# A delta-rule attention and a gated feed-forward layer on one core: the hand-over order of 1879 tasks is replaced by another

## The chip, the cores and the metric

The kernel runs on one core of one Trainium2 chip. The metric is the device time of one execution in microseconds (us). Three runs of the kernel before took 671.13, 673.59 and 679.51 us, so the median is 673.59 us.

A core has five engines that run side by side, each through its own instructions in program order: TensorE (PE in the profile, with its weight loads as PEld), VectorE (DVE), ScalarE (ACT), GpSimd (POOL) and SyncE (SP), which here only issues DMA transfers. An engine that reaches an instruction whose input is not there waits, and all that stands behind it on that engine waits too.

## The reference

```python
# q, k, v: (4, 8, 768, 48); beta: (4, 8, 768)
k_n = k / (np.linalg.norm(k, axis=-1, keepdims=True) + 1e-06)
state = np.zeros((B, H, D, D))
for t in range(S):
    y[:, :, t] = np.einsum('bhd,bhde->bhe', q[:, :, t], state)
    v_old = np.einsum('bhde,bhd->bhe', state, kt)
    state = state + bt[..., None] * np.einsum('bhd,bhe->bhde', kt, vt - v_old)
x = y.transpose(0, 2, 1, 3).reshape(B * S, H * D)     # (3072, 384)
h = x @ w_in                                          # w_in (384, 2048)
out = (h * np.cos(h)) @ w_out                         # w_out (2048, 384)
```

The first half is a recurrence over 768 time steps for 32 pairs of batch and head; the second half is a feed-forward layer with the gate h cos(h). The weights arrive as 64-bit numbers and are narrowed on the chip.

## The kernel before

**Attention, chunk by chunk.** Time is cut into 24 chunks n of 32 steps. For a chunk, TensorE makes the gram matrix of keys with keys and queries (`gram`, L546), sends keys and queries through the state (`state`, L713), multiplies with an inverted triangular matrix (`solve`, L776), updates the state (`update`, L799), forms the output inside the chunk (`within`, L816) and transposes it into features for the feed-forward layer (`features`, L835). These products work on pieces of 48x32, 64x64 or 32x32 rows and columns of the array, the others on 128x128. Between them DVE and ACT carry results out of PSUM: `gram_keys` and `gram_queries` (L557, L580), `right` (L728), `solve_out` (L786), `update_out` (L807), `within_out`, `features_out`.

**The inverse.** The triangular matrices of chunks 2m and 2m+1 are inverted together. The gram goes to DRAM (`gram_put`, L598), comes back in another layout (`gram_get`, L619), is inverted on POOL in seven tasks `inv m,0` to `inv m,6` (L656 and L663; the one of m = 0 runs on DVE), goes to DRAM (`put`, L677) and comes back as `zt` by `get` (L696), which `solve` of the two chunks needs. These transfers are issued by SP, as are the loads of keys, queries and values and the stores.

**Feed-forward, pair by pair.** Each pair p of chunks gives 256 rows. For p = 0 and 1 the hidden layer is plain (`hidden p,f`, L856, 24 matmul instructions each); for p = 0 the output is plain too (`out 0,i,k`, L1001). Later pairs use a scheme with seven products in place of eight: `layer p,s,i` (L975) for the hidden layer and `out p,step,part` (L1058) for the output, with `left`, `layer_out` and `collect` on DVE and ACT as the additions around it. The gate is `turns` (ACT, L896), `rest` (DVE, L903), `cos` (ACT, L912) and `gate` (DVE, L915).

**Weights.** 28 slabs t are loaded (`weights`, SP), narrowed by `split` (ACT), `shift` (DVE) and `add` (POOL, L438). Slabs 0 to 11 are `w_in`, three for each quarter of the hidden layer; `hidden 0,6` is the first to need slabs 9 to 11. Slabs 12 to 27 are `w_out`; `out 0,0,k` needs those up to 15 + 4k, so `out 0,0,3` needs slab 27.

**The order.** All of this is registered as 1879 tasks by `Order.add`, each with the engine, what it depends on, and the tiles that it makes and uses. `Order.LINE` is a string with all task numbers in one sequence, and `Order.run` emits the tasks in that sequence. An engine gets its own tasks in the sequence's order, and a last loop pins every instruction behind the one before it on its engine, so nothing is reordered later. The number of buffers of each kind of tile is fixed: one PSUM tile (two banks) for the attention's small products (`two`), one for `p_kq`, three banks for the hidden layer (`h`), two places of `p_out` for the output, eight buffers `g` in SBUF that gates, weight slabs and some others share.

```python
line = [keys[int(i)] for i in self.LINE.split()]
for key in line:
    emit, deps, makes, uses = self.tasks[key]
    assert deps <= done, key
    ...
    emit()
```

## Time and profile before

| what | value |
|---|---|
| median of three runs (lowest, highest) | 673.59 us (671.13, 679.51) |
| span of the profiled execution, first to last instruction | 670.2 us |
| TensorE busy | 616.5 us, 92% of the span |
| DVE, ACT, POOL busy | 466.5, 242.4, 347.1 us |
| mean granted TensorE clock | 0.995 |
| HBM read, written | 39.24, 10.75 MB |

The span leaves out what lies around the program on the device; the page gives no separate time for it, and the fastest of the three runs is 0.9 us above the span. Most of TensorE's idle time lies in the first 100 us: it is nearly gapless from there to the end.

### The profile page before, as it was taken

Reading aid. Unit: us, or ns where it says so; the run is one execution under the profiler, and the core shown is the slowest. Engines: PE = TensorE matmul, PEld = TensorE weight load, DVE = VectorE, ACT = ScalarE, POOL = GpSimd, SP = SyncE. Lnnn points to the kernel's source line nnn. Section 1 sums busy time; section 2 is a strip of 40 time slices with the busy share of each in tenths; the row PEclk is TensorE's granted clock in tenths of the full one; section 3 lists DMA queues with packets and bytes.
Section 4 is the critical chain, followed back from the end, with each engine's and each line's share of the span. In section 5 each row is a group of like instructions: output and inputs, shape, how many; then the busy total and the mean of one; then the engine's idle time right before and its main releaser. Section 6 shows DMA issues by size and latency. Waiting matters only on the chain.

```text
span 670.2 us, 27723 instructions
## 1 busy us (share of the span) xinstructions
PE 616.5 (92%) x12120; PEld 580.5 (87%) x12120; DVE 466.5 (70%) x892; ACT 242.4 (36%) x416; POOL 347.1 (52%) x734
## 2 busy tenths in 40 slices
PE   4326789999999999999999999999999999999996
PEld 3225779976889999999999999999999999999996
DVE  6872698897577777787767767777776666656662
ACT  3441565650223433334334332333323333332420
POOL 4268778988728658238458484385383382000000
PEclk9999899999899999999999999999999999999999
DMA  8776594464364523544443624623312302000000
GB/s 179 183 177 156 130 228 124 105 110 66 53 103 68 85 54 57 89 88 70 70 83 55 108 35 73 106 39 53 69 27 39 68 2 40 20 2 24 1 25 24
DMA packets 215645, 51.80 MB, mean 77 GB/s; under 512 B 207076, under 2 KB 210420, under 8 KB 215524
## 3 DMA queue, kind: packets, MB, share of 16 engines
q1 hardware_dynamic: 212516, 49.16, 38.0%
q8 instruction: 95, 1.56, 1.0%
q10 hardware_dynamic: 2752, 0.43, 0.4%
q0 software_dynamic: 256, 0.44, 0.2%
q14 instruction: 26, 0.21, 0.1%
HBM read 39.24 MB, written 10.75 MB: 75 GB/s over the span
## 4 chain that ended last, share of the span: by engine, by line
PE 79%; DMA 7%; SPq 4%; POOL 4%; DVE 2%; issue 2%; ACT 0%; ACTq 0%; DVEq 0%; POOLq 0%
PE p_h L975 28%; PE p_out L1058 27%; PE p_h L856 5%; PE p_kq L713 4%; PE p_out L1001 3%; PE p_u L776 3%; PE p_s L799 3%; PE p_kq L816 2%; PE p_g L546 2%; POOL z L663 2%; DMA pairs<-in_moe_w_in_dram 2%; POOL part L656 2%; PE p_o L1058 2%; DMA qp<-in_q_dram 1%; SPq L310 1%
## 5 line engine op out<-in xcount | busy, mean ns | idle before, releaser
L656 POOL TENSOR_TENSOR part<-z,gb 128x126 f32<-128x126 f32 (+22 forms) x341 | 134.6, 395 | 116.1 <-DMA gb<-g_dr 75.0
L663 POOL TENSOR_TENSOR z<-z,part 128x126 f32<-128x126 f32 (+22 forms) x341 | 138.7, 407 | 26.7
L975 PE MATMUL p_h<-x_ffn,w_in 128*128 128x128 f32 x1120 | 143.0, 277 | 0.0
L975 PEld LDWEIGHTS p_h<-x_ffn,w_in 128*128 128x128 f32 x1120 | 134.2, 192 | 1.5
L1058 PE MATMUL p_out<-w_out,g_ffn 128*128 128x192 f32 x672 | 121.8, 330 | 2.0 <-issue 2.0
L1058 PEld LDWEIGHTS p_out<-w_out,g_ffn 128*128 128x128 f32 x672 | 108.7, 191 | 3.3 <-issue 2.1
L896 ACT ACTIVATE turns<-p_h,quarter_turn 128x512 int32<-128x512 f32 x96 | 65.8, 688 | 105.6 <-DVE p_h L994 72.1
L912 ACT ACTIVATE turns<-turns,halfpi 128x512 f32<-128x512 f32 x96 | 68.7, 721 | 64.3 <-DVE turns L903 63.7
L1058 PE MATMUL p_out<-w_sum,g_ffn 128*128 128x192 f32 x496 | 88.7, 329 | 0.0
L903 DVE SCALAR_TENSOR_TENSOR turns<-p_h,turns 128x512 f32<-128x512 f32 x96 | 65.3, 683 | 22.0 <-ACT turns L896 22.0
L1058 PEld LDWEIGHTS p_out<-w_sum,g_ffn 128*128 128x128 f32 x496 | 79.7, 190 | 0.8
L991 ACT COPY g_ffn<-p_h 128x512 f32<-128x512 f32 x60 | 35.0, 584 | 108.8 <-PE p_h L975 108.7
L1074 DVE TENSOR_TENSOR g_ffn<-g_ffn 128x512 f32<-128x512 f32 x88 | 62.3, 715 | 10.0 <-PE p_out L1058 8.9
L915 DVE TENSOR_TENSOR g_ffn<-turns,p_h 128x512 f32<-128x512 f32 x96 | 64.6, 677 | 6.6 <-ACT turns L912 6.5
L994 DVE TENSOR_TENSOR p_h<-g_ffn,p_h 128x512 f32<-128x512 f32 x60 | 41.5, 692 | 30.5 <-PE p_h L975 23.7
L467 POOL TENSOR_TENSOR knrm<-ksum,halves 128x16 f32<-128x16 f32 (+1 forms) x14 | 36.2, 2590 | 41.5 <-DVE ksum L455 41.5
L1108 DVE SCALAR_TENSOR_TENSOR o<-p_out,o 128x192 f32<-128x192 f32 x74 | 25.2, 353 | 35.4 <-PE p_out L1058 33.9
L856 PE MATMUL p_h<-x_ffn,w_in 128*128 128x128 f32 x384 | 47.3, 282 | 2.3 <-POOL part L656 2.1
L856 PEld LDWEIGHTS p_h<-x_ffn,w_in 128*128 128x128 f32 x384 | 45.8, 197 | 3.3 <-issue 2.2
L975 PE MATMUL p_h<-x_sum,in_sum 128*128 128x128 f32 x320 | 41.6, 277 | 0.0
L786 DVE TENSOR_TENSOR u<-p_u,bz 128x384 f32<-128x384 f32 x48 | 24.4, 550 | 21.9 <-PE p_u L776 21.8
L975 PEld LDWEIGHTS p_h<-x_sum,in_sum 128*128 128x128 f32 x320 | 38.7, 192 | 0.5
(110 smaller groups left out, 767.2 us busy)
## 6 DMA issues: line engine op xcount, KB each, us to landing
pairs<-in_moe_w_in_dram SPq DMA_DIRECT2D x12, 512.0 KB
pairs<-in_moe_w_out_dram SPq DMA_DIRECT2D x16, 384.0 KB
gb<-g_dr SPq DMA_DIRECT2D x22, 256.0 KB
vp<-in_v_dram SPq DMA_DIRECT2D x96, 48.0 KB
out_dram<-o SPq DMA_DIRECT2D x23, 192.0 KB
kp<-in_k_dram SPq DMA_DIRECT2D x128, 24.0 KB
z_dr<-z SPq DMA_DIRECT2D x11, 256.0 KB
zt<-z_dr SPq DMA_DIRECT2D x88, 32.0 KB
```

The costliest lines, as they stand in the source:

```text
L467: nc.gpsimd.tensor_tensor(out=scales[m][2][:, part], in0=sums[m, part.start][:, 0:n], in1=halves[:, 0:n], op=ALU.pow,)
L656: eng.tensor_tensor(out=part, in0=z[:, 0:rows, j, None].to_broadcast(shape), in1=a[:, j, None, j + 1 :].to_broadcast(shape), op=ALU.mult,)
L663: eng.tensor_tensor(out=behind, in0=behind, in1=part, op=ALU.subtract)
L856: nc.tensor.matmul(p_h[:, i], w_in[:, t, (4 * k + i) * 128 : (4 * k + i + 1) * 128], xts[p][:, t, unit * 128 : (unit + 1) * 128], start=(t ...
L896: nc.scalar.activation(turns[p, f], hidden_of(p, f), AF.Identity, bias=quarter_turn, scale=TURN)
L903: nc.vector.scalar_tensor_tensor(out=r, in0=hidden_of(p, f), scalar=TURN, in1=t, op0=ALU.mult, op1=ALU.subtract,)
L912: nc.scalar.activation(r, r, AF.Sin, bias=halfpi, scale=2.0 * math.pi)
L915: nc.vector.tensor_tensor(out=place(p, f), in0=step_of(rests.pop((p, f)), f), in1=step_of(hidden_of(p, f), f), op=ALU.mult,)
L975: nc.tensor.matmul(p_h[:, e], in_sum[:, odd_tile, 4 * s + e] if a == "s" else w_in[:, a, f * 128 : (f + 1) * 128], x_sums[p][:, unit] if b ...
L994: nc.vector.tensor_tensor(out=block(p, s, 0, 1) if i == 3 else p_h, in0=block(p, s, *one), in1=p_h, op=ALU.add,)
L1058: nc.tensor.matmul(p_o, left(p, part, a)[:, e % 4], right(e, b), start=(e == 0), stop=(e == FT // 2 - 1), skip_group_check=True,)
L1074: nc.vector.tensor_tensor(out=left(p, s, to), in0=left(p, s, one), in1=left(p, s, two), op=op)
```

## The change

Only the string `LINE` is replaced. Every task, its instructions, its dependences and all buffers are as before; the tasks stand in another sequence, which came out of a new annealing run that was told the length of TensorE's switches between kinds of products and which buffer each tile gets.

```diff
     LINE = """
-0 1767 1 2 14 10 11 12 3 7 4 37 5 42 15 72 6 38 13 39 16 43 73 40 1768 1771 17 44 19 96 75 1769 97
...
-1759 1758 1743 1760 1763 1761 1762 1764 1765 1766
...
+1741 1744 1739 1748 1671 1740 1746 1749 1750 1743 1751 1753 1756 1752 1754 1755 1757 1759 1745 1747
+1758 1760 1763 1764 1761 1765 1762 1766
 """
```

Translated back to task names, these are the places that matter later on.

TensorE, from chunk 0's update to the eleventh feed-forward task:

```
before  update 0, within 0, gram 4, features 0, state 1, solve_half 1, hidden 0,0, between 1, solve 1,
        update 1, within 1, turn 5, hidden 0,2, gram 5, state 2, features 1, turn 6, hidden 0,4,
        out 0,0,0, solve 2, hidden 0,6, update 2, within 2, hidden 0,8, features 2, hidden 0,10, ...
after   update 0, within 0, gram 4, state 1, features 0, solve_half 1, between 1, solve 1, hidden 0,0,
        update 1, hidden 0,2, within 1, turn 5, gram 5, hidden 0,4, state 2, features 1, hidden 0,6,
        turn 6, hidden 0,8, solve 2, update 2, within 2, hidden 0,10, features 2, hidden 0,12, ...
```

POOL, from the first slab to slab 27 (`norms` is a power on POOL, 1.7 to 3.3 us):

```
before  add 0, norms 1, norms 1, add 1 2 3 5 4, norms 2, inv 1,0-1, add 6, inv 1,2-3, add 7, inv 1,4, add 10,
        inv 1,5-6, add 13 8 12 14 15 9 11, norms 3, add 16 17, inv 2,0-1, add 18 19 20, inv 2,2-3, norms 4,
        add 22 21, inv 2,4, add 24 23, inv 2,5, add 26 25 27, inv 2,6, norms 5, inv 3,0 ...
after   norms 1, norms 1, add 0, norms 2, add 5 3 2 6 1 4, inv 1,0-3, add 7, inv 1,4-5, add 8, inv 1,6,
        add 10 11 9, norms 3, add 14 16, inv 2,0, add 12 13, inv 2,1, add 15, inv 2,2, add 17 18 20 19 21,
        inv 2,3-4, add 22 23, inv 2,5-6, add 25 26 24 27, inv 3,0 ...
```

In the middle part, gram and state products, which stand apart before (`state 8` and `gram 11` with a feed-forward product between them), stand side by side in seven more places (`gram 10, state 8, gram 11`). The seven output products of a pair and the eight layers of the next are interleaved in another rhythm: in 13 places a single short layer (8 matmul instructions) stands between the end of one output product and the start of the next; before, in one place. On SP the stores, loads and the transfers of the inverse pass one another in many places.

## Prediction

> **What bounds the kernel now.** First the busy time by stretches (PE, PEld, DVE, ACT, POOL in us, then the granted clock, the DMA share, GB/s):

> ```profile
> core 0: us, PE busy (x) PEld busy (x) DVE busy (x) ACT busy (x) POOL busy (x), PEclk, DMA share, GB/s
> 0.00:66.00 66.00, 28.16 (x843) 23.47 (x844) 42.48 (x118) 22.78 (x41) 37.68 (x58) 1.00 0.76 173
> 66.00:100.00 34.00, 28.14 (x707) 25.15 (x707) 26.62 (x43) 19.80 (x37) 25.71 (x41) 0.95 0.77 180
> 100.00:143.00 43.00, 42.73 (x834) 39.66 (x833) 37.41 (x67) 25.92 (x48) 36.72 (x62) 1.00 0.50 108
> ...
> 165.60:168.40 2.80, 0.85 (x16) 0.67 (x5) 1.71 (x2) 0.00 (x0) 2.33 (x7) 1.00 0.20 30
> 168.40:171.90 3.50, 3.50 (x72) 2.95 (x71) 0.34 (x1) 0.00 (x0) 2.95 (x8) 0.51 0.34 59
> ...
> 216.00:430.00 214.00, 214.00 (x4382) 205.74 (x4381) 159.53 (x304) 78.41 (x132) 121.64 (x280) 1.00 0.44 74
> ```

> TensorE is full from 100 us to the end but for three short stalls; before that it idles some 44 us. So the change can act in three ways: the start, TensorE's own length, and stalls.

> Next the chain of waits between 60 and 100 us (start, length, what), which says what held the start back:

> ```profile
> 83.13 5.14 DMA z_dr<-z
> ...
> 97.45 0.89 PE p_s L799 x32
> ```

> Before this stands an unbroken row of `POOL part L656` and `POOL z L663`: inverse 1, ended at 83.1, then `put 1`, `get 2`, and chunk 2's update at 97.45, with TensorE gapless afterwards. POOL's waits show what interrupts it there:

> ```profile
> POOL w_in L438 <- DVE w_in L434: 19.4, 5, 12.4
> ...
> POOL w_out L438 <- DVE w_out L434: 5.9, 5, 1.9
> ```

> Last the chain between 505 and 560 us, for the price of a switch:

> ```profile
> 514.39 0.72 PE p_g L546 x49
> ...
> 516.33 2.80 PE p_out L1058 x16
> 519.13 0.84 PE p_g L546 x62
> ...
> 521.06 2.60 PE p_out L1058 x16
> ...
> 547.96 1.31 PE p_kq L713 x85
> 549.27 1.50 PE p_out L1058 x8
> ```

> The same 16 instructions take 2.80 after a product on small pieces and 2.60 after a 128x128 one; every other product shows this 0.20. A gram with its state behind it takes 516.33 - 514.39 = 1.94; apart they take 0.84 and 1.31.

> **TensorE's own length.** Decoding both strings, TensorE changes between piece sizes 185 times before and 173 times after; gram and state stand side by side in 11 places before, 18 after. One joining saves 0.84 + 1.31 - 1.94 = 0.21 and one 0.20: 0.41 by these pieces, 0.35 by starts in the timeline, so seven save 2.5 to 2.9. Going the other way, one more visit to 32x32 and one `update` parted from its `within` cost 0.2 each. Laid end to end with the row's durations, the products from `out 0,0,3` to the end come to 513.2 before and 510.4 after: **-2.8**. No trace shows a state followed at once by the next gram; if that saves only the 0.20, the term is -1.7; at most it is -3.2.

> **The start.** The first stretch hardly moves. The DVE order puts `sum 0,1` ahead, which starts `norms 0` some 2 us later (10.9 for 9.1), but `gram_keys 0` waited to 13.3 anyway; both gram transfers leave some 0.4 us earlier; two DVE tasks (`gram_queries 2` 0.41, `scale 1,1` 1.0) now stand before inverse 0's last task, so `put 0` leaves at about 36.0 (35.5 before); `get 0` no longer queues behind `gram_get 1` on SP and leaves at 39.4 (40.6). `solve_half 0` comes to about 44.8 (46.0).

> Then POOL decides. Seven slabs now precede inverse 1 on POOL; their `shift`s stand on DVE behind inverse 0 (34 to 35 us), so inverse 1 starts at about 50.5 for 47.9. From there to the end of `add 27` POOL took 140.9 - 47.9 = 93.0. The new order puts `inv 2,6` in front of it (6.4 + 0.6 idle), takes `norms 4` (2.9) and `add 6` (1.3) out, and with slabs prepared early most of 9.6 us in which POOL waited for slabs between (2.9, 1.7, 1.9, and several of 0.8) can go: I take 6.8. That gives 93.0 + 7.0 - 4.2 - 6.8 = 89.0, so slab 27 at 139.5, and `out 0,0,3`, which needs it, at 139.9 for 142.9: **-3.0**. TensorE's path agrees: slabs 10, 11, 9 follow inverse 1 (50.5 + 28.0 + 2.6 for two slabs + idle = 81.8, three slabs: 85.8), releasing `hidden 0,6`; from it to `out 0,0,3` are 51.7 of products and one wait of 1.2 for `solve_out 2`, together 138.7. Bounds: none of POOL's waits saved, 146.3 and +3.4; all saved, TensorE's own path, 138.7 and -4.2.

> **Stalls that go.** `out 1,1,0` stood still from 166.07 for 1.95 with nothing to wait for ("issue"), and the trace has a packet of the instruction queue at 165.1, just before; the next 3.5 us ran at a clock of 0.51, and products there are 1.9 longer. This hangs on where TensorE is in its code, not on an order that I can read: I count half, **-1.9**. `solve 6` and `solve 16` waited 1.57 and 0.99 for `zt`, and products around them took 2.0 longer (`solve 6` 1.36 for 0.73): **-4.5** if both go. By the new positions `zt` of chunk 6 is there 5.7 before its solve.

> [...]

> **Stalls that come.** (a) `zt`. Chunk 8's solve moves 6.4 of work later, but `gram_keys 9` now follows `layer_out 2,0,4` on DVE, and `gram_put 9` queues on SP behind `get 6`, `get 7` and `blocks 10`. With `gram_get 4` at 191.5, 4.8 to inverse 4, 28.0 for it and two `norms` of 2.9 that now stand inside, `put 4` leaves at 230.9; 5.5 to `get 8` and 3.8 to use give 240.2, and TensorE wants it at 139.9 + 99.0 = 238.9: a wait of 1.3. The same walk leaves chunks 18 and 22 within a microsecond of waiting, the others 3 to 7 spare. I take two waits of 1.3 with 0.6 of slower products each: +3.8, between 0 and 8. (b) Cover behind products. For each product I compared the work between it and the product whose result it needs through DVE or ACT with the durations on that way plus 0.2 for each hand-over. After `out 0,1,3` the margin is under 0.5 us in 8 places before, in 44 after: the joined grams have 1.16 of cover for 1.24 (a gram must wait until DVE has read the other out of `two`), 13 output products have 0.89 for 0.75 of `collect`, in one place before. The 8 places waited 0.0. What can spoil it is a DVE task in front: DVE is busy 159.53 of 214. As none of the 8 waited, I take 0.05 each: +2.2; ends 0 and, at 0.3 each, 13. Together **+6.0**.

> **Sum.** 670.2 - 2.8 - 3.0 - 1.9 - 4.5 + 6.0 = 664.0 for the profiled span. The median stands 3.4 above that span (673.59 to 670.2), so 667.4: I predict **667 us**. ACT and the remaining SP moves count nothing: ACT is busy 36%, stores are waited for by nobody until the last, whose place is unchanged.

> **Rivals.**
> - *The start gains all and nothing comes back*: 670.2 - 4.2 - 2.8 - 3.9 - 4.5 + 3.4 = 658.2. For it: POOL's waits in the start are real. Against: 36 new tight places. 0.20.
> - *Only the switches count*, POOL's waits stay, stalls move: 673.6 - 2.2 = 671.4. For it: POOL's path to slab 27 is 7.0 longer. 0.20.
> - *Lost cover makes it slower*: one DVE task of 0.68 in front in all 44 places is 30 us, 697. It decides (over 687) from 20 / 44 = 0.45 us a place. For it: `scale 9` (1.1 to 1.5) now stands right before `right 13`, whose solve has 0.13 of margin. Against: the 8 places of before. 0.12.
> - *Forecast*: 0.48.

> The range 656 to 682 takes in the first two rivals and (b)'s upper half. Under 2% from 673.6, 660.1 to 687.1, a measurement of this kernel hardly tells a change from none. The first rival falls mostly below: faster 0.20; forecast and second within: 0.69; slower 0.11.

> **What would show it.** Right: `add 27` ends near 139.5 and `out 0,0,3` starts near 140; TensorE busy from there some 2.8 shorter; no wait at `solve 6`; in TensorE's waits a few entries for `zt` and small ones for `g`/`tt` (L580) and `o` (L1108). Wrong: `add 27` after 143, or waits for DVE adding to over 10 us after 160, or an idle start much shorter than 40 us.

## The result and the profile after

The kernel after takes 705.8 us (median of four runs, 704.25 to 709.49), the kernel before 674.32 beside it (four runs): **1.051 times as long, interval 1.046 to 1.057**. Another pair of runs on another chip gave 1.045 (1.041 to 1.049). The forecast was 667, the range ended at 682.

First the busy time by stretches of the kernel after (PE, PEld, DVE, ACT, POOL in us, then the granted clock, the DMA share, GB/s). The third and fourth row are one stand-still and the 3.5 us behind it:

```profile
core 0: us, PE busy (x) PEld busy (x) DVE busy (x) ACT busy (x) POOL busy (x), PEclk, DMA share, GB/s
0.00:66.00 66.00, 24.93 (x776) 20.88 (x776) 38.65 (x111) 21.63 (x40) 34.15 (x53) 0.99 0.73 172
66.00:100.00 34.00, 29.59 (x704) 27.08 (x688) 21.14 (x40) 17.93 (x34) 26.39 (x47) 0.81 0.63 140
...
444.88:447.12 2.24, 0.01 (x2) 0.00 (x0) 2.14 (x8) 1.44 (x2) 0.00 (x0) 1.00 0.47 68
447.12:450.60 3.48, 3.48 (x32) 3.31 (x32) 1.05 (x3) 0.00 (x0) 0.00 (x0) 0.52 0.16 24
216.00:430.00 214.00, 200.89 (x4053) 192.97 (x4057) 146.76 (x277) 69.04 (x117) 124.44 (x286) 0.96 0.40 66
```

In the stretch from 216 to 430 us, where TensorE was busy for all 214.00 before, it now stands still for 13.1 and gets through 4053 matmul instructions in place of 4382. DVE and ACT are less full than before, POOL is hardly fuller (124.44 for 121.64). TensorE's waits behind 148 us (engine, line, what was late; us in total, times, longest) say that nothing was late:

```profile
PE p_g L544 <- issue: 9.1, 4, 2.5
PE p_kq L711 <- issue: 8.4, 5, 2.6
PE p_out L1056 <- issue: 3.0, 2, 2.0
PE p_out L1056 <- ACT g_ffn L989: 2.3, 1, 2.3
PE p_u L774 <- issue: 1.5, 2, 1.3
...
```

Before, the same view has two lines:

```profile
PE p_u L776 <- DMA zt<-z_dr: 2.6, 2, 1.6
PE p_out L1058 <- issue: 2.0, 1, 2.0
```

"Issue" is a wait for nothing that the profile shows. After, there is no entry for `zt`, and none for DVE. The one entry for ACT is of the same kind, as its place below tells. The chain of waits shows one of them from near (start, length, what): a gram, a state, and a stop inside the second gram.

```profile
442.47 0.72 PE p_g L544 x49
...
443.25 1.16 PE p_kq L711 x68
444.41 0.48 PE p_g L544 x34
444.88 2.23 issue
447.12 0.58 PE p_g L544 x23
447.70 4.27 PE p_out L1056 x16
```

A gram does not depend on anything between its first and its last instruction, so it is not data that stops it there. The `out` behind it takes 4.27 for the 2.80 of before: that is the clock of 0.52.

What does stop it is in the DMA queues (packets, MB, share of 16 engines):

```profile
q8 instruction: 95, 1.56, 0.9%
```

TensorE has 24,388 records of its own in this trace, weight loads included, and the 95 packets have 16,384 bytes each: about 256 instructions a packet, 256.7 by division. Numbering the records from the first one, **every stand-still of over 0.25 us behind 102 us, 17 of them, lies at number 256k + 449 or 450**. Before, the two that the waits view calls issue, 0.3 us at 140 and 2.0 at 166, are at 256 * 17 + 449 and 256 * 20 + 449; so is one of 2.1 at 64 us that the view puts down to POOL (256 * 5 + 449). Worked out from the trace of after, the five from 330 to 510 us that are longer than 1.5:

```
idle from, to (us)   idle   TensorE instruction   packet k of queue q8, its transfer (us)
337.75  339.89       2.13   256 * 46 + 449        46: 337.19 to 338.31
365.36  367.05       1.68   256 * 50 + 449        50: 364.29 to 365.63
390.84  392.95       2.12   256 * 54 + 449        54: 390.59 to 391.47
444.88  447.12       2.23   256 * 62 + 449        62: 444.31 to 445.71
501.78  504.30       2.52   256 * 70 + 450        70: 501.95 to 502.83
```

(The wait put down to ACT is the stop from 289.14 to 291.48, at 256 * 39 + 449.) Each time packet k lands inside or just ahead of the stop, and TensorE goes on about 1.4 us after it has landed. The reading is that TensorE has run out of code; the shifts in the experiments test it. Where the time went, from TensorE's row of products laid end to end with the same durations as in the prediction (us). These are the two profiled executions, whose spans are 670.2 and 707.7; the one after is the slowest of its four runs, and the medians lie 31.5 apart:

| | before | after | difference |
|---|---|---|---|
| `out 0,1,0` starts | 148.2 | 153.4 | +5.2 |
| from there: products end to end | 506.6 | 503.9 | -2.7 |
| idle at 256k + 449 (places) | 2.0 (1) | 25.3 (16) | +23.3 |
| idle elsewhere | 2.6 | 0.0 | -2.6 |
| products slower than end to end | 4.2 | 18.9 | +14.7 |
| sum, to the last product's start | 663.6 | 701.5 | +37.9 |

### The profile page after: what moved, and what is told of

The parts are those of the page before. It is cut to its first block, busy times and chain, and to the rows that moved or that the text cites. A ratio compares the mean times of both kernels' runs of the same rounds, so it can differ in the third digit from the quotient of the medians.

```text
span 707.7 us, 27694 instructions
## 1 busy us (share of the span) xinstructions
PE 629.5 (89%) x12120; PEld 593.4 (84%) x12120; DVE 457.3 (65%) x892; ACT 239.1 (34%) x416; POOL 341.3 (48%) x734
## 4 chain that ended last, share of the span: by engine, by line
PE 83%; DMA 5%; issue 5%; DVE 3%; POOL 1%; ACT 1%; SPq 1%; DVEq 0%
PE p_h L973 29%; PE p_out L1056 29%; PE p_h L854 5%; PE p_kq L711 4%; PE p_out L999 3%; PE p_u L774 3%; PE p_s L797 3%; PE p_kq L814 3%; PE p_g L544 2%; DMA qp<-in_q_dram 2%; DMA pairs<-in_moe_w_in_dram 2%; PE p_o L1056 1%; PE p_z L833 1%; SPq L308 1%; DVE w_in L432 1%
## 5 line engine op out<-in xcount | busy, mean ns | idle before, releaser
L654 POOL TENSOR_TENSOR part<-z,gb 128x126 f32<-128x126 f32 (+22 forms) x341 | 132.5, 389 | 188.4 <-DMA gb<-g_dr 118.1
L661 POOL TENSOR_TENSOR z<-z,part 128x126 f32<-128x126 f32 (+22 forms) x341 | 135.8, 398 | 26.7
L973 PE MATMUL p_h<-x_ffn,w_in 128*128 128x128 f32 x1120 | 147.4, 282 | 0.7 <-issue 0.7
L973 PEld LDWEIGHTS p_h<-x_ffn,w_in 128*128 128x128 f32 x1120 | 140.6, 198 | 1.4 <-issue 0.7
L1056 PE MATMUL p_out<-w_out,g_ffn 128*128 128x192 f32 x672 | 127.3, 339 | 5.3 <-issue 3.0
L1056 PEld LDWEIGHTS p_out<-w_out,g_ffn 128*128 128x128 f32 x672 | 112.5, 197 | 7.0 <-issue 5.8
L1056 PE MATMUL p_out<-w_sum,g_ffn 128*128 128x192 f32 x496 | 92.8, 335 | 0.0
L1056 PEld LDWEIGHTS p_out<-w_sum,g_ffn 128*128 128x128 f32 x496 | 81.5, 194 | 1.2
L854 PE MATMUL p_h<-x_ffn,w_in 128*128 128x128 f32 x384 | 48.1, 286 | 0.4 <-DVE g_ffn L913 0.4
L854 PEld LDWEIGHTS p_h<-x_ffn,w_in 128*128 128x128 f32 x384 | 46.3, 200 | 1.9 <-DVE g_ffn L913 0.6
L711 PE MATMUL p_kq<-st,kq_t 48*32 48x48 f32 x2944 | 34.6, 215 | 13.3 <-issue 13.3
L711 PEld LDWEIGHTS p_kq<-st,kq_t 48*32 48x32 f32 x2944 | 30.5, 106 | 16.3 <-issue 15.4
```

Of the source, the lines that this page charges most:

```text
L654: eng.tensor_tensor(out=part, in0=z[:, 0:rows, j, None].to_broadcast(shape), in1=a[:, j, None, j + 1 :].to_broadcast(shape), op=ALU.mult,)
L661: eng.tensor_tensor(out=behind, in0=behind, in1=part, op=ALU.subtract)
L711: nc.tensor.matmul(p_kq[quarter(b), par, a, j], kq_t[rows48(par), a, b * NP + j], st[rows48(par), b // 2, j, b % 2], start=(j == 0 and a = ...
L854: nc.tensor.matmul(p_h[:, i], w_in[:, t, (4 * k + i) * 128 : (4 * k + i + 1) * 128], xts[p][:, t, unit * 128 : (unit + 1) * 128], start=(t ...
L973: nc.tensor.matmul(p_h[:, e], in_sum[:, odd_tile, 4 * s + e] if a == "s" else w_in[:, a, f * 128 : (f + 1) * 128], x_sums[p][:, unit] if b ...
L1056: nc.tensor.matmul(p_o, left(p, part, a)[:, e % 4], right(e, b), start=(e == 0), stop=(e == FT // 2 - 1), skip_group_check=True,)
```

## The experiments

**Theory A, code supply.** A new packet must be there by instruction 256k + 449, where the stops lie. As an estimate, fitted to the lengths of the stops in before and after, it can be used some 3.75 us after TensorE passes 256k + 153 (single stops of over 0.4 us behind 102 us in after end 3.2 to 5.8 us behind that point, half of them within 4.2); so 296 instructions in less than 3.75 us run TensorE out of code. Wide products are far slower than that (an `out` has 16 instructions in 1.3 us), but a gram with its state and the next gram has 128 + 256 + 128, two packets, in 2.7 us (2.68 from 286.46 in after, where the stop comes only behind the row). Whether such a row stops depends on where the boundary falls in it. **Theory B, lost cover:** the second gram waits until DVE has read the first out of the one tile of its kind. **Theory C:** the half clock has a cause of its own. "The count" in the expectations is theory A's rule applied to an order of tasks.

### Moving the code, not the order

The order of before is kept and TensorE gets 32 (later 64 and 16) tiny products on a constant, at 4.9 us, while it waits for the first keys. The texts below call them 16x16; the trace has them as 128 rows by 8 columns.

```diff
+    for _ in range(32):
+        nc.tensor.matmul(flat_out[0:H, 0:H], halves[:, 0], halves[:, 1])
+
     lasts, done = {}, [len(nc.cur_bb.bb.instructions)]
```

> The kernel before with its order untouched; only 32 products of 16x16 on a constant stand ahead of TensorE's first instruction, while it waits for the first keys: 128 more instructions in its code, so that everything behind them lies half a packet of 256 further on. Theory A (code supply: the traces show TensorE's code coming in 95 packets of 16,384 bytes, 256 instructions each, and every long stand-still at instruction 256k + 449; a stretch of 296 instructions that takes less than 3.75 us runs TensorE out of code): the same products now meet those boundaries elsewhere; counted over the order of before this gives about 14 stand-stills that sum to 21 us, each of some 2 us followed by about 3.5 us at half clock, so +27 to +34: 700 to 707, with the waits put down to nothing (issue). Theory B (DVE comes too late behind the joined products of the new order, code plays no part): the order is that of before, 672 to 676, no new waits. Theory C (the half clock has another cause, such as load on the chip): as B.

> The same with 64 such products, 256 more instructions: a whole packet, so that every product lies at the same place inside its packet as before. Theory A: the stand-stills of before and no others (out 1,1,0 near 166 and one near 64), 672 to 678. If instructions at the front cost something in themselves, or longer code does, this run shows more than the run with 128: over 705. Theory B: 672 to 676.

> The kernel before with 16 products of 16x16 ahead of TensorE's first instruction: 64 more instructions, half of the earlier shift. Theory A: the count over the order of before gives 11 stand-stills and 13 us (14 and 21 us for 128, which measured 1.05), so 1.025 to 1.033 of the kernel before, 685 to 695. If 128 was slow for another reason than where the boundaries fall, this run has no reason to lie between: about 1.00 or about 1.05.

Measured: 128 instructions **1.051 (1.044 to 1.057)**, 704.3 us against 668.7; 256 instructions 1.006 (1.003 to 1.009); 64 instructions 1.019 (1.016 to 1.023). Half a packet costs as much as the whole change, a whole packet next to nothing. TensorE's waits behind 148 us, first with 128, then with 256 instructions:

```profile
PE p_kq L713 <- issue: 17.2, 8, 2.9
PE p_out L1058 <- DVE turns L903: 2.0, 1, 2.0
...
```

```profile
PE p_u L776 <- DMA zt<-z_dr: 1.7, 2, 0.9
PE p_out L1058 <- issue: 1.3, 1, 1.3
```

The same products in the same order stop eight times inside a `state` in the one and not at all there in the other; with 128 the stops lie at 256k + 449 again, 128 instructions earlier in the order (the 2.0 put down to DVE is one of them). Of the time that the 128 cost, 12.7 us lie ahead of `out 0,1,0`, where three stops of 2.0 to 3.2 us come at 85, 117 and 146 us. One of them in the chain of the kernel with 128, and the stretches around it:

```profile
437.52 0.72 PE p_g L546 x49
...
438.30 0.96 PE p_kq L713 x56
439.26 2.95 issue
442.21 0.37 PE p_kq L713 x21
```

```profile
439.26:442.21 2.95, 0.00 (x2) 0.00 (x0) 1.23 (x2) 0.07 (x1) 0.00 (x0) 1.00 0.88 148
442.21:445.70 3.49, 3.49 (x36) 3.42 (x36) 0.00 (x0) 0.00 (x0) 0.00 (x0) 0.67 0.79 108
```

In before the same `gram 18` and `state 16`, from 412.79 on, run through without a stop. This settles A against B and C: no order, no buffer and no dependence changed. The dose with 64 came out lower than expected (the expectation said 1.025 to 1.033); its stops behind 100 us sum to 14.0 us, near the 13 counted, but less half clock follows (6.9 us of slower products for 11.7 with 128).

### Joining and opening the rows

Four of the seven joinings alone, made in the kernel before (TensorE's order):

```diff
-state 14, layer 6,0,0, out 4,6,0, gram 17, out 4,6,1
+state 14, gram 17, layer 6,0,0, out 4,6,0, out 4,6,1
-state 16, out 5,6,0, out 5,6,1, gram 19
+state 16, gram 19, out 5,6,0, out 5,6,1
-state 18, out 6,6,0, out 6,6,1, gram 21
+state 18, gram 21, out 6,6,0, out 6,6,1
-state 20, out 7,6,0, out 7,6,1, gram 23
+state 20, gram 23, out 7,6,0, out 7,6,1
```

> The kernel before with four of the seven new joinings alone: gram 17, 19, 21 and 23 put right behind state 14, 16, 18 and 20; one or two feed-forward products of each place move behind the gram; nothing else moves. Theory A: five stand-stills, 9 us by the count, two of them near state 16 and the grams from 410 us on, with about 12 us of half clock behind them, less 1.6 for eight switches: about 693 (686 to 698), put down to issue. Theory B (the second gram waits until DVE has read the first out of the one tile of its kind): waits in front of grams 17, 19, 21, 23 put down to DVE, at most 1.2 each, so 672 to 678.

And the reverse, the seven rows of after opened:

```diff
-gram 8, state 6, gram 9, layer 2,0,2, out 1,3,0, out 1,3,1
+gram 8, state 6, layer 2,0,2, out 1,3,0, gram 9, out 1,3,1
...
-gram 22, state 20, gram 23, out 7,6,0, out 7,6,1, layer 9,0,1
+gram 22, state 20, out 7,6,0, out 7,6,1, gram 23, layer 9,0,1
```

> The kernel after with the seven new gram-state-gram rows opened: two feed-forward products (one at gram 21) moved in between the state and the second gram; nothing else moves. Theory A: the count of stand-stills after 100 us falls from 20 to 10 us, five places of half clock of some 2.4 go, 14 more switches cost 2.6: about 686 (681 to 693). Theory B: the gain is what DVE waits in front of those grams were worth; the profile of after has under 2 us of them, so 704 to 709.

Measured: joined **1.019 (1.015 to 1.024)**, 682.1 against 668.7; opened 1.037 (1.033 to 1.042), 693.7. The ranges in the texts start from a kernel before of about 674, and here it takes 668.7: joined is 13.4 over it, inside the 12 to 24 that theory A expects from there, and opened is 25 over it, where A's 681 to 693 means 7 to 19. After measured 1.045 and 1.051, so opening gained 5 to 10 us, not the 20 that A counted; by the times alone that is little more than B's nothing, and it is the trace that tells them apart. The waits behind 148 us of the joined kernel:

```profile
PE p_g L545 <- issue: 5.8, 4, 2.5
PE p_g L545 <- DVE tt L579: 2.5, 3, 1.6
PE p_out L1057 <- issue: 2.0, 2, 1.4
...
```

Both mechanisms are here: 8.5 us at packet boundaries (9.0 counted), and 2.5 of theory B, where a gram really waits for DVE's `gram_queries` (L579), up to 1.6 at `gram 23`. Where the second gram has waited for DVE, the boundary behind it costs less (0.34 at 526.7 us): the two share the same time. Products end to end are 1.5 shorter, as four joinings at 0.41 should make it. The opened kernel halves the stops, 25.3 to 13.3 in its 13 places that are left, and pays with 2.7 of switches and 6.4 of other waits, which the moved products caused:

```profile
PE p_kq L712 <- issue: 8.7, 6, 2.3
PE p_h L974 <- DVE x_sum L936: 2.0, 2, 1.2
PE p_g L545 <- issue: 1.9, 2, 1.1
PE p_out L1000 <- POOL w_out L437: 1.8, 1, 1.8
PE p_out L1057 <- DVE g_ffn L914: 1.7, 1, 1.7
...
```

What is left stops at `state`, in rows that are dense without the second gram.

### Is the new order only unlucky?

The tiny products again, 32 of them, in the kernel after.

> The kernel after with 32 products of 16x16 ahead of TensorE's first instruction: 128 more instructions. Theory A: the count over the order of after gives 20 to 23 us of stand-stills wherever the boundaries fall (22 here, 20 unshifted), since a row of gram, state and gram is longer than two packets: 1.04 to 1.07 of the kernel before, other stand-stills than in the profile of after but as many. If the order of after only meets the boundaries by bad luck, as before would when shifted, the run comes down to 1.00 to 1.02.

> The kernel after unchanged, to stand beside the next run on the same chip: 1.045 to 1.057 of the kernel before.

Measured: 1.055 (1.051 to 1.059), and unshifted beside it 1.045 (1.041 to 1.049). With 128 more instructions the stops lie in other products, and there are about as many: 21.0 us in 15 places behind `out 0,1,0`, for 21.6 in 16 unshifted in these runs. The order of before depends on where the boundaries fall; that of after loses at the two places tried, and no third was tried.

### The two halves apart

The tasks up to about 160 us from one order, all others from the other.

> The order of after up to out 1,0,1 (its first 426 tasks), all other tasks in the order of before: the new start alone. Every product behind it lies at the same place in TensorE's code as before. Theory A: out 0,0,3 ends some 5 us later than before, as in the profile of after, and nothing is added behind it: about 5 us over the kernel before. Theory D (the late start is what costs: buffers and the transfers of the inverse stay late all the way): most of the 35 us, over 25.

> The order of before up to solve 4 (its first 437 tasks, 159 us), all other tasks in the order of after: the new rest alone. Theory A: the 13 or so stand-stills of after behind 170 us are all here, out 0,0,3 is as before: 27 to 32 us over the kernel before. Theory D: 0 to 8 us over it.

Measured: the new start alone 1.021 (1.017 to 1.025), the new rest alone 1.035 (1.031 to 1.040), some 24 us. The rest has 22.2 us at boundaries in 15 places and 0.2 elsewhere, as A says; the sum comes out under the expected 27 because less half clock follows than in after (11.0 us of slower products for 18.9). The start was expected to cost 5 and cost 14: `out 0,0,3` begins at 147.4, 4.5 later than before, and then `solve 5` waits 7.2 for `right 5`. That wait belongs to the splice, not to either order: 24 tasks that stand early in before and late in after all come right behind the cut, and on DVE they push `right 5` from 165.8 to 180.4. Behind it not one stop at a boundary is left (0.0 us), with before's products at before's places.

### The start

`out 0,0,3` was to come at 139.9 and came at 148.0. Five kernels took candidates away. On their own:

```diff
 POOL (new_start_pool)   -add 6, add 1, add 4, inverse 1,0-3
                         +inverse 1,0-1, add 6, add 1, inverse 1,2, add 4, inverse 1,3
 DVE (new_start_pool)    -shift 6, shift 1, shift 4, scale 2,0, between_out 0, solve_out 0, update_out 0
                         +between_out 0, shift 6, shift 1, solve_out 0, shift 4, update_out 0, scale 2,0
 POOL (after_slab27)     -inverse 2,5, inverse 2,6, add 25, add 26, add 24, add 27
                         +inverse 2,5, add 25, add 26, add 24, add 27, inverse 2,6
```

> new_start with seven tasks moved: on POOL add 6, 1 and 4 go from ahead of inverse 1 to behind its second and third part; on DVE shift 6, 1, 4 and scale 2,0 go behind between_out 0, solve_out 0 and update_out 0. If the start is late because DVE prepares slabs ahead of chunk 0 (solve 0 waits 3.6 there) and POOL adds three slabs ahead of inverse 1 (53 for 48 us), inverse 1 begins 3 to 5 us earlier and the run is 2 to 5 us faster than new_start. If slab 27 is held by POOL's own waits for shifts later on (13 us between 50 and 150), the run equals new_start within 1 us.

> The kernel after with one task of POOL moved: inverse 2's last part behind add 25, 26, 24 and 27 (as in before). In the profile of after, the load of slab 27 leaves at 143.2 us for 131.2 in before, in the moment in which add 25 ends and frees a buffer, and add 25 stands behind inverse 2's last part. If that is what holds out 0,0,3, the load leaves near 138, add 27 ends near 144 and out 0,0,3 starts near 142.5 for 148.0; 4 to 6 us less than the kernel after if nothing else becomes late (about 0.7%). Rival (TensorE's own late start holds it: solve 0 and state 1): out 0,0,3 gains under 1.5 us and the time stays within 2 us of after.

Then one after the other, each on top of the last:

```diff
 SP (after_put1)         -weights 15, gram_put 5, put 1, weights 16, gram_get 2, weights 17, get 2
                         +put 1, weights 15, gram_put 5, weights 16, get 2, gram_get 2, weights 17
 DVE (.._solve0)         -shift 1, shift 4, scale 2,0, between_out 0
                         +between_out 0, shift 1, shift 4, scale 2,0
 POOL (.._slab27)        as in after_slab27
```

> The kernel after with two of SP's tasks moved: put 1 ahead of weights 15 (which waits there for a buffer) and get 2 ahead of gram_get 2. If SP's queue alone holds the start, put 1 leaves near 85.2 for 87.9, get 2 near 90.2 for 92.8, solve 2 starts 2.5 us earlier and out 0,0,3 near 145.5 for 148.0. If TensorE's own path is as late, solve 2 moves by its wait alone, 0.4 to 1.4, and out 0,0,3 stays above 146.5. The stand-stills behind 150 us stay as they are: 1.04 to 1.055 of the kernel before.

> after_put1, and on DVE shift 1, shift 4 and scale 2,0 go behind between_out 0, so that solve 0 waits about 1 us for 3.6. If both paths together hold the start, out 0,0,3 starts 2 to 3 us earlier than in after_put1, near 144. If POOL, whose add 1 and add 4 in front of inverse 1 now come later, takes it back (inverse 1 begins after 54), out 0,0,3 does not gain.

> after_put1_solve0, and on POOL inverse 2's last part goes behind add 25, 26, 24 and 27. If slab 27 is what is late next, add 27 ends near 144 and out 0,0,3 starts near 143 (142.9 in before); if it was never the limit, out 0,0,3 is as in after_put1_solve0 within 0.7 us.

Measured, from the profiles (us; "waits" are TensorE's in front of that product):

| kernel | time, to before | `solve 0` waits | inverse 1 begins | `put 1` | `get 2` | `solve 2` (waits) | `add 27` ends | `out 0,0,3` |
|---|---|---|---|---|---|---|---|---|
| before | 1 | 0.7 | 47.9 | 83.1 | 88.3 | 92.4 (0.0) | 140.9 | 142.9 |
| after | 1.051 | 3.6 | 52.9 | 87.9 | 92.8 | 98.9 (0.4) | 149.4 | 148.0 |
| after, again | 1.045 | 3.9 | 50.8 | 84.9 | 91.0 | 96.6 (1.4) | 148.1 | 146.8 |
| after_slab27 | 1.047 | 3.6 | 52.4 | 86.4 | 92.7 | 98.1 (1.7) | 147.5 | 148.5 |
| new_start_pool | 1.029 | 0.8 | 51.3 | 90.4 | 95.5 | 101.8 (0.9) | 153.3 | 151.4 |
| after_put1 | 1.036 | 4.1 | 50.3 | 82.1 | 85.5 | 95.3 (0.0) | 145.3 | 144.3 |
| after_put1_solve0 | 1.045 | 0.7 | 53.5 | 85.3 | 89.8 | 97.0 (1.0) | 148.8 | 146.9 |
| after_put1_solve0_slab27 | 1.045 | 0.7 | 54.8 | 87.3 | 90.7 | 99.8 (0.0) | 147.2 | 148.8 |

A caution first: these are single executions. `out 0,0,3` comes at 139.9 to 142.9 in the four profiled kernels that share the start of before (before, before_joined, before_eased, new_rest), and at 146.8 to 148.0 in the four that share that of after (after, after again, after_open, new_start).

Slab 27 was no limit: its `add` came 0.6 to 1.9 earlier and nothing followed (1.047, as after); in after itself `out 0,0,3` begins 1.4 before `add 27` ends. `new_start_pool` met neither of its forecasts: inverse 1 begins 1.2 earlier than in new_start (51.3 for 52.5), but with three slabs added between its parts it ends at 88.3 for 84.7, and the run is 5.6 slower than new_start. Only the moves on SP were followed by an earlier `out 0,0,3`. In after, `put 1` stands behind `weights 15`, which waits until POOL frees a buffer:

```profile
86.42 0.35 SPq L413 DMA_DIRECT2D pairs<-in_moe_w_out_dram  x1
87.45 0.39 SPq L596 DMA_DIRECT2D g_dr<-g  x1
87.89 0.57 SPq L675 DMA_DIRECT2D z_dr<-z  x1
...
92.84 1.82 SPq L694 DMA_DIRECT2D zt<-z_dr  x4
```

Inverse 1 is done at 85.1 and its result leaves at 87.9. With `put 1` ahead, `out 0,0,3` comes at 144.3, and the ratio of 1.036 (1.031 to 1.041) is lower than both of after and just under the forecast 1.04, though its interval meets that of 1.045. Taking the wait from `solve 0` as well gives it back (1.045 on the same chip), as the column of inverse 1 shows: slabs 1 and 4 are prepared later, POOL adds them ahead of inverse 1, and inverse 1 begins 3.2 later. With slab 27's move on top `out 0,0,3` comes 1.9 later still, which neither forecast had; inverse 1 begins 1.3 later there as well. These profiles suggest, and do not show, that two paths take turns in holding the start, DVE and POOL ahead of inverse 1 and SP behind it; the part that one edit freed is about 2.5 of 5.

TensorE's own stops tell where the 5 us stand. In after, chunk 2's update begins at 101.1 for 97.4, so 3.7 are there by then. From it to `out 0,0,3` TensorE stands still twice in after, for 0.74 in `state 3` and 0.75 in `state 4`, both at 256k + 449, and once in before, for 0.28: another 1.2, which is code again. What would free the 3.7 stays open.

### A try at beating both

Before with 7 products moved, so that no dense row meets the boundary near 166 us and the two waits for `zt` get cover:

```diff
-features 4, state 5, out 1,1,0, solve 5, out 1,1,1, update 5, within 5, out 1,2,0, features 5, out 1,2,1
+features 4, out 1,1,0, state 5, out 1,1,1, solve 5, out 1,2,0, update 5, within 5, out 1,2,1, features 5
-solve 6, layer 2,1,0
+layer 2,1,0, solve 6
-solve 16, out 6,2,0
+out 6,2,0, solve 16
```

> The kernel before with 7 of TensorE's tasks moved and nothing else: state 5 behind out 1,1,0, solve 5 behind out 1,1,1, update 5 and within 5 behind out 1,2,0, features 5 behind out 1,2,1, so that no row of small products runs up to the packet boundary near 166 us; solve 6 behind layer 2,1,0 and solve 16 behind out 6,2,0, since both wait for zt. Theory A: the stand-still of 2 us near 166 and the half clock behind it go (2 to 4 us), and 1 to 3 us of the waits for zt: 3 to 7 us faster than the kernel before. Rival: what is late next takes it back, within 2 us of the kernel before.

Measured: 0.9985 (0.9956 to 1.0015), no difference. The idle time at boundaries behind `out 0,1,0` fell from 2.0 to 0.7, but now an `out` waits 2.0 for the output place at 169.8 and `solve 6` still waits 2.0. The rival held: what was late next took it.

The kernels in one table (without those of the start), from `out 0,1,0` on (us; one profile each). The last two columns mostly go together: the more idle time at boundaries, the more time products lose by running slower.

| kernel | time, to before | `out 0,1,0` | products end to end | idle elsewhere | idle at 256k + 449 (places) | slower products |
|---|---|---|---|---|---|---|
| new_start | 1.021 | 152.9 | 506.6 | 12.2 | 0.0 (0) | 5.5 |
| before_eased | 0.9985 | 147.8 | 506.6 | 4.3 | 0.7 (2) | 2.9 |
| before + 256 | 1.006 | 147.1 | 506.6 | 1.7 | 1.3 (1) | 3.1 |
| before | 1 | 148.2 | 506.6 | 2.6 | 2.0 (1) | 4.2 |
| before_joined | 1.019 | 145.2 | 505.1 | 3.7 | 8.5 (7) | 12.7 |
| before + 64 | 1.019 | 151.1 | 506.6 | 0.5 | 9.7 (8) | 6.9 |
| after_open | 1.037 | 155.6 | 506.6 | 6.4 | 13.3 (13) | 5.8 |
| before + 128 | 1.051 | 160.9 | 506.6 | 0.2 | 17.6 (10) | 11.7 |
| after + 128 | 1.055 | 158.8 | 503.9 | 2.2 | 21.0 (15) | 13.0 |
| after, again | 1.045 | 152.1 | 503.9 | 1.0 | 21.6 (16) | 12.9 |
| new_rest | 1.035 | 147.5 | 503.9 | 0.2 | 22.2 (15) | 11.0 |
| after | 1.051 | 153.4 | 503.9 | 0.0 | 25.3 (16) | 18.9 |

## Why the prediction was wrong

**The step that failed** is the code stall at 166: "This hangs on where TensorE is in its code, not on an order that I can read: I count half, -1.9." The first half is true and the second is not. Where TensorE is in its code follows from the order alone: the instructions of each product are in the trace, and so are the packets. And under the stalls that come the prediction has no term for code at all: it let the one stop go by half and put new ones at nothing. The stops of before already stood at 256k + 449, and its profile had 95 instruction packets for some 24,400 instructions. The packet at 165.1, "just before", was also misread: it is of queue q14; the packet of q8, packet 20 for the stop at 256 * 20 + 449, runs from 165.47 to 166.78, into the stop. In place of -1.9 the profiles show +23.3 of idle time and most of the +14.7 of slower products; the shift by 128 shows that the place in the code alone can cost as much, with the order untouched.

**The joining of gram and state** (-2.8) was right in size: 2.7 shorter behind `out 0,1,0`. It is also part of what made the stops: opening the seven rows takes 12 of the 25.3 us away. The saving of 0.41 a joining was counted, and that the joined row hands TensorE 512 instructions in 2.7 us was not.

**The waits for `zt`** (-4.5, then +3.8): 2.6 us of waiting in front of `solve 6` and `solve 16` went, and in after none came; a later TensorE gives every transfer more time, so this says little on whether they would have come in a kernel without stops. `new_rest` and after_again wait 0.2 and 1.0 elsewhere than at boundaries, which speaks against 3.8. The walk to chunk 8 also has a slip: 191.5 + 4.8 + 28.0 + 2 * 2.9 is 230.1 and not 230.9, so that its wait would be 0.5 and not 1.3.

**Thin cover** (+2.2, rival at 697): the time of the rival is near the measured one, and its mechanism is not it. In after the places outside boundaries add up to 0.0 of idle time. Where the four joinings were made in before, 2.5 us of such waits did come, so the margins were read rightly; in after the stops may give DVE the time, which no run shows.

**The start** (-3.0): wrong in sign, +5.1. Three terms of it failed. POOL's waits for slabs were to shrink from 9.6 (the waits view from 46 to 142 us has 8.8) to 2.8; POOL's waits from 50 to 150 us in after are

```profile
POOL w_out L436 <- DVE w_out L432: 10.8, 6, 3.2
POOL w_in L436 <- DVE w_in L432: 1.3, 2, 1.0
```

with two more of 0.8 and 0.4 for another of DVE's tasks. "With slabs prepared early" left out that a load waits for one of eight buffers which POOL's own adds free: slab 27 leaves at 143.2, when `add 25` ends, 131.2 before. TensorE's path was counted by the slabs of `hidden 0,6` (85.8, and it began at 91.5), without `put 1`, which left 2.8 after the end of inverse 1, behind a load on SP. And `solve 0` waited 3.6 for DVE, with a stop of 3.4 in `state 1` behind it, another boundary (256 * 4 + 449). Of the tests named in the prediction, `add 27` after 143 was the one that said so.

On the clock, the prediction had the one stop of 1.95 us with 3.5 us at 0.51 behind it. With more of them: of the eight stops of 2.0 to 2.6 us behind 100 us in after, seven are followed by 3.5 us at 0.50 to 0.72 and one at 1.00; the one of 1.68 is followed by 0.74, those of 1.44 and 1.33 by 1.00. What went with the half clock in these traces stands in the last section. Most boundaries show no stop: behind `out 0,1,0` TensorE passes 76 of them in each kernel, and stops at one in before and at 16 in after. Each of the seven gram-state-gram rows of after has a stop inside it or right behind it.

## What to carry to other kernels

Number the instructions of the engine that bounds the kernel and lay the packets of its code beside them. Here the idle time put down to nothing fell at the same place of every packet, 256k + 449, where some 300 instructions had passed in under about 4 us, and in before 64 or 128 instructions more at the front put other products on those places, at 1.9% and 5.1%. Where a trace shows the same, suspect code first, and shift the code without touching the order to see whether the stops move. Put slow, wide products between rows of many small ones (in after that took the stops from 25.3 to 13.3 us, for 2.7 of switches and 6.4 of other waits), and do not join such rows to save a switch of 0.2 us when a stop costs 2 and the half clock behind it some 1.7 more (an estimate: half of the 3.41 us for which the clock stays at 0.5). On an engine that only issues transfers, look at what the entry ahead of a moved transfer waits for: `put 1` left 2.8 us after the end of inverse 1, behind a load that waited for a buffer.
